# Second 512 rows of x in a gated MLP on one core: eight transposing DMAs, or plain loads turned by TensorE

## The chip, the cores and the metric

The kernel runs on one core of a Trainium2 chip. The metric is the device time of one execution in microseconds (us); of several runs the median counts. All times of instructions come from one profiled execution of the kernel before.

## The reference

```python
B, S, Dm, Df = 1, 2048, 1024, 3584        # all inputs bf16, output bf16
def reference(x, w_gate, w_up, w_down):
    g = jnp.einsum("bsd,df->bsf", x, w_gate)
    u = jnp.einsum("bsd,df->bsf", x, w_up)
    h = jax.nn.gelu(g, approximate=True) * u
    return jnp.einsum("bsf,fd->bsd", h, w_down)
```

## The kernel before, in words

**Passes and units.** The 2048 rows of x are done in two passes of 1024 rows. A pass first makes the hidden layer `hT` for its rows (fourteen units, each with 256 of the 3584 hidden columns) and then multiplies it by `w_down` (`down`). The two 512-row halves of a pass are called c = 0 and c = 1; `xT[0]` and `xT[1]` hold them transposed, the contraction on the partitions.

**Seven products in place of eight.** A unit is a 2x2 block product, for gate and for up, done with seven block products and sums of operands. `sums_t` makes the sums of x: `t1` to `t4`, and `tb`, a cast; they are made once for a pass. `sums_s` makes those of the unit's weights: `s1` to `s4` and `sa`. Sums are kept in fp32r. The block products are the calls of `product` and `first_product` in `unit`; each is four matmuls of 128x512 for gate and four for up, all issued at line 111 in the helper `matmul`.

**The very first unit is plain.** Unit 0 of pass 0 is done without the sums, by `plain`, because the operands are still coming. Five warm-up matmuls (line 484) run first. Then `turn` transposes the four row blocks of the first 512 rows on TensorE (line 434, eight 128x128 transposes for each block, into banks 4 to 7), and VectorE or ScalarE copies each block to `xT[0]` (line 435). `plain(bank[0:4], 0, ...)` follows, then `plain(bank[4:8], 1, ...)`. The second 512 rows arrive already transposed: the helper `transposing` (line 438) issues eight transposing DMAs on SyncE's queue, one for each 128 columns of x, behind the loads of the first rows (`xn`) and of unit 0's weights (`wf`).

**Orders.** TensorE, VectorE, GpSimd and SyncE carry out their instructions in the order of the program; in this opening stretch ScalarE does too. DMAs on SyncE's queue are therefore issued in the order written, and one that waits holds back those behind it. Unit 1's weights (`w = load_w(1, nc.scalar, pinned=True)`) come by ScalarE's queue, issued behind its copy of the second row block. Unit 2's weights also come by ScalarE's queue: `aside(-1)` in unit 1 issues them behind the two snapshots `p1` of `first_product`. Later weights come by SyncE's queue.

**Who makes the sums.** In unit 1 VectorE makes `t` and `s`, ScalarE casts `tb` and `sa`. From unit 2 on GpSimd makes `s1` to `s4` one unit ahead (`make_s(ahead, pool)`). In pass 0 GpSimd also makes the sums of `w_down` in `keep`, tile `m` (one block j of 128 hidden rows of both halves for each unit, the last three at the end, two of them in a weight buffer, where the profile calls the tile `w`); `store_made` writes them to DRAM (`td`) a unit later, and `down` reads them back. The loads of `w_down` that `down` needs (`raw`, line 319) stand on SyncE's queue, some of them behind the last of these stores.

**Pools.** `k` has 52 slots of 2 KB for a partition and holds the row blocks `xn`, the sums, the snapshots and the gelu results; `w` has three weight buffers. A new tile waits until the readers of the slot's last tile are done.

Of the kernel before, what the change touches and what calls it, by code (L numbers as in the profile page):

```python
# [10 lines left out]
def kernel(  # L11
# [23 lines left out]
    nc = tc.nc  # L35
    ENG = mybir.EngineType
    ORDER = {ENG.SP, ENG.DVE, ENG.Pool, ENG.PE}
    P = nc.NUM_PARTITIONS
    bf16 = mybir.dt.bfloat16
# [6 lines left out]
    x2 = x.flatten_outer_dims()  # L46
# [4 lines left out]
    NKB = Dm // P  # L51
# [3 lines left out]
    N = 512  # L55
    NS = N // P
# [19 lines left out]
    def new_x():  # L76
        return [xpool.tile([P, NKB, N], bf16, name=f"xT{c}") for c in range(2)]
# [36 lines left out]

    def load_w(u, queue=nc.sync, pinned=False):
        f0 = u * 2 * P
        w = wpool.tile([P, 2, NKB, 2 * P], bf16, name="w")
        for i, src in enumerate((w_gate, w_up)):  # L120
            got = queue.dma_start(
                out=w[:, i],
                in_=src[:, f0 : f0 + 2 * P].rearrange("(ko ki) f -> ki ko f", ki=P),
            )
            if queue is not nc.sync and not pinned:
                tc.keep_in_program_order(got)
        return w

# [7 lines left out]
    def sums_t(xT):  # L136
        K = range(KH)
        lo, hi = [[xT[c][:, k] for k in K] for c in range(2)], [
            [xT[c][:, KH + k] for k in K] for c in range(2)
        ]  # L140
        return Sums(
            how={
                "t1": lambda q: [new(dve, lo[1][k], lo[0][k], SUB, "t1") for k in K],
                "t2": lambda q: [new(dve, hi[1][k], q["t1"][k], SUB, "t2") for k in K],
                "t3": lambda q: [new(dve, hi[1][k], lo[1][k], SUB, "t3") for k in K],
                "t4": lambda q: [new(dve, hi[0][k], q["t2"][k], SUB, "t4") for k in K],
                "tb": lambda q: [cast(hi[1][k], "tb") for k in K],
            }
        )

    def sums_s(w, eng):
        GU = range(2)
        sh = [P, KH, P]
        a11, a21 = [[w[:, i, :KH, h : h + P] for i in GU] for h in (0, P)]
        a12, a22 = [[w[:, i, KH:, h : h + P] for i in GU] for h in (0, P)]
        return Sums(
            how={
                "s1": lambda q: [new(eng, a21[i], a22[i], ADD, "s1", sh) for i in GU],
                "s2": lambda q: [new(eng, q["s1"][i], a11[i], SUB, "s2", sh) for i in GU],
                "s3": lambda q: [new(eng, a11[i], a21[i], SUB, "s3", sh) for i in GU],  # L160
                "s4": lambda q: [new(eng, a12[i], q["s2"][i], SUB, "s4", sh) for i in GU],
                "sa": lambda q: [cast(a22[i], "sa", sh) for i in GU],
            }
        )
# [257 lines left out]
    def load_x(c):  # L422
        t = []
        for i in range(NS):
            xn = slot([P, Dm], bf16, "xn")
            r0 = c * N + i * P
            nc.sync.dma_start(out=xn, in_=x2[r0 : r0 + P, :])
            t.append(xn)
        return t

    def turn(xT, xn, c, i, copy):
        tp = bank[4 + i].bitcast(bf16).rearrange("p (k r) -> p k r", k=NKB)
        for ko in range(NKB):
            nc.tensor.transpose(tp[:, ko, :], xn[i][:, ko * P : (ko + 1) * P], ident)
        copy(out=xT[c][:, :, i * P : (i + 1) * P], in_=tp)

    def transposing(xT, c, ko, r0):
        nc.sync.dma_start_transpose(
            out=xT[c][:, ko, :], in_=x2[r0 : r0 + N, ko * P : (ko + 1) * P]
        )  # L440

    def load_wf(queue, k0, k1):
        for i, src in enumerate((w_gate, w_up)):
            got = queue.dma_start(
                out=wf[:, i, k0:k1],
                in_=src[k0 * P : k1 * P, 0 : 2 * P].rearrange(
                    "(ko ki) f -> ki ko f", ki=P
                ),
            )
            if queue is not nc.sync:  # L450
                tc.keep_in_program_order(got)

    xT = new_x()
    xn0 = load_x(0)
    wf = wpool.tile([P, 2, NKB, 2 * P], bf16, name="w")
    for k0, k1 in ((0, 2), (2, 5), (5, NKB)):
        load_wf(nc.sync, k0, k1)
    for ko in range(NKB):
        transposing(xT, 1, ko, N)

    def plain(ps, c, kos, parts=1):
        n = N // parts
        for k in range(kos.start, kos.stop, 2):
            for part in range(parts):
                cols = slice(part * n, (part + 1) * n)
                for p, (j, i) in zip(ps, [(j, i) for j in range(2) for i in range(2)]):
                    for ko in (k, k + 1):
                        matmul(
                            p[:, cols],
                            wf[:, i, ko, j * P : (j + 1) * P],  # L470
                            xT[c][:, ko, cols],
                            ko == 0 and part == 0,
                            ko == NKB - 1,
                        )

    def finish(ps, c):
        for j in range(2):
            times(j, c, gelu(ps[2 * j]), ps[2 * j + 1])

    on_dve, on_act = nc.vector.tensor_copy, nc.scalar.copy  # L480
    t = sums_t(xT)
    with tc.manual_schedule(engines={ENG.Activation}):
        for _ in range(NWARM):
            nc.tensor.matmul(bank[3], lhsT=warm[:, :P], rhs=warm, start=True, stop=True)
        for i in range(NS):
            turn(xT, xn0, 0, i, on_act if i == 1 else on_dve)
        w = load_w(1, nc.scalar, pinned=True)
        s = sums_s(w, dve)
        plain(bank[0:4], 0, range(0, 2), parts=2)
        plain(bank[0:4], 0, range(2, NKB))  # L490
        t.make("t1")
        finish(bank[0:4], 0)
        s.make("s1", "s2")
        t.make("t2", "t3", "tb")
        s.make("s3", "sa")
        plain(bank[4:8], 1, range(NKB))
        finish(bank[4:8], 1)
# [8 lines left out]
    for ip in range(NPASS):  # L506
        for u in range(1 if ip == 0 else 0, NU):
            js = making(u) if ip == 0 else []

            def prepare():  # L510
                nonlocal ahead
                nxt["w"], nxt["s"] = ahead, None
                if u + 1 < NU:
                    nxt["s"] = make_s(ahead, pool)
                if u + 2 < NU:
                    ahead = load_w(u + 2)
                if ip == 0:
                    fetch_wd(making(u + 1))
                    for j in making(u - 1):
                        store_made(j)  # L520
                for j in js:
                    keep(j, j != js[0])

            def aside(part):
                nonlocal ahead
                if ahead is None:
                    ahead = load_w(2, nc.scalar)
                if part == 0 and "s4" not in s:
                    s.make("s4")
                    t.make("t4")  # L530

            def ahead_of_p4():
                if u + 1 < NU:
                    nxt["p1"] = first_product(even if u % 2 else odd, xT, nxt["w"])

            e = odd if u % 2 else even
            p1 = nxt.pop("p1", None) or first_product(e, xT, w)
            unit(u, (e, cc, dd), xT, w, s, t, p1, prepare, aside, ahead_of_p4, ip == 0 and u == 1)
            if u + 1 < NU:
                w, s = nxt["w"], nxt["s"]  # L540

        last = ip == NPASS - 1
        got, nxt = {}, {}

        def more(step):

            nonlocal ahead
            if last:
                return
            if step == 0:  # L550
                xT[:] = new_x()
                for j in making(NU - 1):
                    store_made(j)
            if step >= 16 and step % 2 == 0 and step // 2 - 8 < len(moves):
                c, ko = moves[step // 2 - 8]
                transposing(xT, c, ko, (2 * (ip + 1) + c) * N)
            if step == 50:
                got["w"], ahead = load_w(0), load_w(1)
            if step == 58:
                got["s"] = make_s(got["w"], dve)  # L560
            if step == 62:
                got["t"] = make_t(xT)

        down(ip, even + cc, dd + odd, last, more)
        even, odd, cc, dd = odd, even, dd, cc
        if not last:
            w, t, s = got["w"], got["t"], got["s"]
# [29 lines left out]
```

## Time and profile before

| what | value |
|---|---|
| median of 3 runs | 555.94 us (555.9 to 557.38) |
| profiled execution, its own time | 557.38 us |
| its span, first to last instruction | 555.5 us |
| TensorE busy | 539.2 us, 97% |
| VectorE, ScalarE, GpSimd busy | 325.1, 243.5, 279.4 us |
| TensorE's waits for DMAs of `raw` | 10.5 us, 3 times, the longest 9.3 us |
| mean DMA rate | 168 GB/s |

The profiled execution is the longest of the three runs shown; 1.9 us of its time lie outside the span. A busy share is an average: what a change in the opening is worth depends on what the opening hands on, and to which engine.

### The profile page before, as it was taken

The numbers are of one execution on the slowest core, as the hardware profiler recorded it, in microseconds if no ns is written. First come the engines' busy times: TensorE is split into PE (matmuls) and PEld (weight loads), VectorE is DVE, ScalarE is ACT, GpSimd is POOL, SyncE is SP. The second block draws the span as 40 slices with busy tenths as digits, with TensorE's granted clock in tenths as the row PEclk, the third lists the DMA queues.
The fourth block names the chain that finished last, engine by engine and source line by source line (L and its number), as shares of the span: only waits on it lengthen the run. The fifth ranks groups of instructions, "written<-read, shape, count | busy, mean of one in ns | idle before, by whom it ended". The sixth has DMA issues, their size and how long they took to land.

```text
span 555.5 us, 7315 instructions
## 1 busy us (share of the span) xinstructions
PE 539.2 (97%) x2405; PEld 380.1 (68%) x2405; DVE 325.1 (59%) x490; ACT 243.5 (44%) x427; POOL 279.4 (50%) x248
## 2 busy tenths in 40 slices
PE   8999999999999939999999999999999999999997
PEld 5477776676777514788877777766767776478885
DVE  3884555545554892468675445555555548866730
ACT  2555554555555201045435555545555551114541
POOL 0069999999999620000059666777777700000000
PEclk9999999999999969999999999999999999999999
DMA  9884767766634589999925333222222049563751
GB/s 212 164 229 124 201 188 196 201 189 171 170 101 165 203 295 353 265 252 250 327 65 150 100 106 99 77 76 77 76 77 76 0 141 370 190 225 84 223 194 53
DMA packets 108133, 93.28 MB, mean 168 GB/s; under 512 B 17216, under 2 KB 92992, under 8 KB 108096
## 3 DMA queue, kind: packets, MB, share of 16 engines
q1 hardware_dynamic: 103936, 90.72, 56.7%
q10 hardware_dynamic: 4160, 2.10, 1.5%
q8 instruction: 19, 0.31, 0.2%
q14 instruction: 18, 0.15, 0.1%
HBM read 74.45 MB, written 15.20 MB: 161 GB/s over the span
## 4 chain that ended last, share of the span: by engine, by line
PE 61%; DMA 3%; POOL 1%; issue 1%; ACT 0%; SPq 0%; POOLq 0%
PE bank L111 61%; DMA raw<-in_w_down_dram 2%; POOL w L93 1%; DMA td<-w 1%; POOL m L93 1%; DMA td<-m 1%; ACT st L398 0%; SPq L280 0%; POOLq L93 0%
## 5 line engine op out<-in xcount | busy, mean ns | idle before, releaser
L93 POOL TENSOR_TENSOR s<-w 128x512 fp32r<-128x512 bf16 x100 | 116.9, 1189 | 158.0 <-DVE t L90 86.6
L111 PE MATMUL bank<-t,s 128*128 128x512 f32 x648 | 157.0, 398 | 0.0
L111 PEld LDWEIGHTS bank<-t,s 128*128 128x128 f32 x648 | 121.8, 188 | 27.6
L107 ACT COPY p<-bank 128x512 f32<-128x512 f32 x124 | 71.5, 589 | 113.4 <-PE bank L111 113.3
L111 PE MATMUL bank<-xT,w 128*128 128x512 bf16 (+1 forms) x504 | 117.2, 380 | 0.0
L90 DVE TENSOR_TENSOR hT<-g,bank 128x512 bf16<-128x512 f32 x112 | 76.7, 687 | 55.7 <-ACT g L178 48.1
L90 DVE TENSOR_TENSOR sum<-bank,p 128x512 f32<-128x512 f32 x54 | 37.3, 691 | 88.9 <-PE bank L111 87.5
L111 PEld LDWEIGHTS <-w 128*128 128x128 bf16 x504 | 45.8, 99 | 59.4 <-issue 12.9
L178 ACT ACTIVATE g<-sum 128x512 f32<-128x512 f32 x81 | 51.3, 633 | 55.1 <-DVE sum L90 53.5
L111 PE MATMUL bank<-raw,hT 128*128 128x512 bf16 x224 | 51.7, 392 | 10.5 <-DMA raw<-in_w_down_dram 10.5
L111 PE MATMUL bank<-q 128*128 128x512 f32 x240 | 59.0, 389 | 0.0
L111 PE MATMUL bank<-t,sa 128*128 128x512 f32 x216 | 58.7, 413 | 0.0
L93 POOL TENSOR_TENSOR s<-w,s 128x512 fp32r<-128x512 bf16 x50 | 57.5, 1168 | 0.0
L93 POOL TENSOR_TENSOR s<-s,w 128x512 fp32r<-128x512 f32 x50 | 57.2, 1164 | 0.0
L111 PE MATMUL bank<-tb,s 128*128 128x512 f32 x216 | 53.3, 389 | 0.0
L111 PEld LDWEIGHTS bank<-q 128*128 128x128 f32 x240 | 45.1, 188 | 9.3
L111 PEld LDWEIGHTS <-hT 128*128 128x128 bf16 x224 | 22.3, 100 | 39.5 <-issue 15.3
L111 PEld LDWEIGHTS bank<-t,sa 128*128 128x128 f32 x216 | 40.7, 188 | 10.6
L107 ACT COPY u<-bank 128x512 f32<-128x512 f32 x62 | 35.8, 589 | 24.3 <-PE bank L111 24.3
L111 PEld LDWEIGHTS bank<-tb,s 128*128 128x128 f32 x216 | 40.6, 188 | 8.4
L102 ACT CAST tb<-raw 128x512 fp32r<-128x512 bf16 x28 | 17.2, 628 | 63.0 <-DMA raw<-in_w_down_dram 29.7
L90 DVE TENSOR_TENSOR q<-hT 128x512 fp32r<-128x512 bf16 x56 | 42.1, 752 | 3.4 <-PE bank L111 3.4
(43 smaller groups left out, 460.1 us busy)
## 6 DMA issues: line engine op xcount, KB each, us to landing
raw<-in_w_down_dram SPq DMA_DIRECT2D x80, 256.0 KB, 3.6
q<-td SPq DMA_DIRECT2D x60, 256.0 KB, 5.0
w<-in_w_gate_dram SPq DMA_DIRECT2D x25, 512.0 KB, 4.4
w<-in_w_up_dram SPq DMA_DIRECT2D x25, 512.0 KB, 5.9
td<-m SPq DMA_DIRECT2D x12, 768.0 KB, 4.5
w<-td SPq DMA_DIRECT2D x6, 1024.0 KB, 9.0
out_dram<-st SPq DMA_DIRECT2D x32, 128.0 KB, 1.7
td<-w SPq DMA_DIRECT2D x2, 768.0 KB, 3.8
```

The lines of the kernel that those rows point to most:

```text
L90: nc.vector.tensor_tensor(out=out, in0=a, in1=b, op=op)
L93: nc.gpsimd.tensor_tensor(out=out, in0=a, in1=b, op=op)
L102: nc.scalar.copy(out=t, in_=src)
L107: nc.scalar.copy(out=t, in_=ps)
L111: nc.tensor.matmul(ps, lhsT=lhs, rhs=rhs, start=start, stop=stop, skip_group_check=True)
L178: nc.scalar.activation(g, src, ACT.Gelu_apprx_tanh)
```

## The change

The second 512 rows of x come like the first: four plain loads of 128 rows each (`load_x(1)`, tile `xn`), turned by 32 transposes on TensorE and copied to `xT[1]`, two blocks by VectorE and two by ScalarE. The transposes stand inside the plain product of the first rows, two blocks after its first four contraction blocks and two after its sixth. Unit 1's weights move from ScalarE's queue to SyncE's, behind these loads. On VectorE `s1` of unit 1 now stands ahead of unit 0's gated product `hT`, and `s2` behind `t2`. After this opening the instructions of all engines are the same in both kernels, in the same order.

```diff
-    for ko in range(NKB):
-        transposing(xT, 1, ko, N)
+    xn1 = load_x(1)
+    w = load_w(1)
...
-    t = sums_t(xT)
+    s, t = sums_s(w, dve), sums_t(xT)
...
             turn(xT, xn0, 0, i, on_act if i == 1 else on_dve)
-        w = load_w(1, nc.scalar, pinned=True)
-        s = sums_s(w, dve)
         plain(bank[0:4], 0, range(0, 2), parts=2)
-        plain(bank[0:4], 0, range(2, NKB))
+        plain(bank[0:4], 0, range(2, 4))
+        for i in range(2):
+            turn(xT, xn1, 1, i, on_act if i % 2 else on_dve)
+        plain(bank[0:4], 0, range(4, 6))
+        for i in range(2, NS):
+            turn(xT, xn1, 1, i, on_act if i % 2 else on_dve)
+        plain(bank[0:4], 0, range(6, NKB))
         t.make("t1")
+        s.make("s1")
         finish(bank[0:4], 0)
-        s.make("s1", "s2")
-        t.make("t2", "t3", "tb")
+        t.make("t2")
+        s.make("s2")
+        t.make("t3", "tb")
         s.make("s3", "sa")
         plain(bank[4:8], 1, range(NKB))
         finish(bank[4:8], 1)
```

The other lines of the diff write out the helpers `transposing` and `load_wf` where they were called (the transposing DMAs of pass 1's rows stay as they are) and drop the parameter `pinned`.

## The prediction

> **What bounds the kernel now.** I read the page's totals first, then the chain that ended last, then the opening and GpSimd in the timeline.
>
> ```profile
> PE 539.2 (97%) x2405; PEld 380.1 (68%) x2405; DVE 325.1 (59%) x490; ACT 243.5 (44%) x427; POOL 279.4 (50%) x248
> ```
>
> TensorE is busy for 97%, so time added to it anywhere looks like time added to the end. The chain of waits, in order of time, corrects this:
>
> ```profile
> 184.88 1.17 POOL m L93
> ...
> 193.18 1.60 POOL w L93
> ...
> 197.93 4.34 DMA td<-w
> ...
> 202.70 11.26 DMA raw<-in_w_down_dram
> 213.96 0.04 issue
> 214.00 338.08 PE bank L111 x1504
> ```
>
> Columns are start, length, what. From 214 us to the end TensorE never waits. Before that the chain is not TensorE's: GpSimd's sums of `w_down`, their stores, and the loads of `raw` behind those stores. TensorE sits idle there for 10.5 us (9.35 in one piece). So a delay of TensorE in the opening reaches the end only if GpSimd's chain is delayed too. Where does that chain begin?
>
> ```profile
> 24.84 0.37 ACTq L121 DMA_DIRECT2D w<-in_w_gate_dram  x1
> 25.24 0.61 ACTq L121 DMA_DIRECT2D w<-in_w_up_dram  x1
> 32.09 1.16 POOL L93 TENSOR_TENSOR s<-w 128x512 fp32r<-128x512 bf16 x1 [30.79 <-DMA w<-in_w_gate_dram]
> 33.91 1.15 POOL L93 TENSOR_TENSOR s<-w 128x512 fp32r<-128x512 bf16 x1 [0.66 <-DMA w<-in_w_up_dram]
> ```
>
> GpSimd starts on unit 2's weights when they land. The timeline of GpSimd shows no idle time from 33.91 until 180.41: eight sums of `s` and three of `m` fill 12.60 us, exactly TensorE's time for a unit (its sets of `bank<-t,s` start at 38.77, 51.37, 63.97). Whatever delays the landing of unit 2's up weights passes through to 214 us. These two DMAs are issued at 24.84 because they stand on ScalarE's queue behind the `p1` snapshots (the second starts at 24.83), which wait for TensorE's first product of unit 1. TensorE in the opening:
>
> ```profile
> 1.19 2.32 PE L484 MATMUL bank<-warm 128*128 128x512 bf16 x5 [1.19 <-DVE warm L418]
> 3.30 1.91 PE L434 MATMUL bank<-ident,xn 128*128 128x128 bf16 x16
> 6.35 1.89 PE L434 MATMUL bank<-ident,xn 128*128 128x128 bf16 x16 [1.14 <-DMA xn<-in_x_dram]
> 8.03 18.49 PE L111 MATMUL bank<-xT,w 128*128 128x256 bf16 x88
> 33.64 1.90 PE L111 MATMUL bank<-xT,w 128*128 128x512 bf16 x8
> ```
>
> After 8.03 there is no gap. The eight transposing DMAs held nobody up on TensorE, so their removal gives it nothing back.
>
> **The transposes.** 32 are added in that dense stretch, all ahead of the `p1` snapshots. The only row for such a matmul is that of the first rows: 16 in 1.91 us, each 0.31 long, so (1.91 - 0.31) / 15 = 0.107 us apart. That is a slow stretch: the warm-up matmuls of 512 columns are (2.32 - 0.63) / 4 = 0.42 us apart, against (1.90 - 0.38) / 7 = 0.217 at 33.64. (The granted clock reads 1.00 in both, so the pace is read from the spacing.) In the trace the pace doubles at 10.1 us, inside the first `plain` matmuls; the new transposes start at about 12.5. In the slow stretch a transpose takes a quarter of a 512-column matmul, which its 128 columns explain; weight loads hide. At the fast pace a quarter is 0.054. So the bounds are 32 x 0.054 = 1.7 us and 32 x 0.107 = 3.4 us. A gain is excluded: nothing leaves TensorE, and no gap is left to fill. I take 0.055, nearest to the row of the same stretch: **+1.8 us**.
>
> Here the Trainium skill speaks against this change. The page "TensorE: Matmul & The Clock Gate", section "Part 4: PE-mode transpose", says that transposes take about 275 ns in a kernel and that the full clock does not engage for them. The row has 314 ns for the length of one, but neighbours overlap. If the slow spacing held for them at any clock, the sum would be the 3.4 us of the upper bound; the 16 here that stood inside the busy time just before the pace doubled speak against it.
>
> **Do the rows arrive in time?** The loads take the places of the transposing DMAs, whose first is issued at 6.32. The DMA windows show 324 to 330 GB/s from 5 to 8 us, and the first 2 MB (x and `wf`) land by about 10.2. At 0.8 us for each 256 KB the four blocks land near 11.0, 11.8, 12.6 and 13.4. TensorE asks for the first at 10.82 + 8 x 0.216 = 12.54 and for the third at 12.54 + 0.9 + 1.7 = 15.2. Cover: 1.5 and 2.6 us; without it, TensorE waits by the difference. `w` follows by 16.7; `s1` wants it near 20. No cost.
>
> **The copies.** ScalarE's copy of a block took 1.01 us, VectorE's 0.69. Behind the last transposes TensorE has eight matmuls (1.73 us), while the last copy needs about 0.2 to drain and 1.01 on ScalarE. Cover 0.4 us, cost nothing. ScalarE loads its gelu table behind the copies (1.28 us), so unit 0's gelu is about 1 us later relative to TensorE; its banks are asked for 5 us later.
>
> **VectorE.** Before, `t1` is done at 16.3, having waited 4.5 us for the transposing DMAs. Now it starts when the last copy ends, near 17.4. From there 21 operations, 0.61 us apart (18 took 10.95 from 16.25), stand before unit 0's last-but-one `hT` is written: 30.3. That `hT` frees bank 5, which TensorE wants for the second half of `s1` x `t1` at 26.17 + 1.8 + 1.85 + 0.93 = 30.7. Cover 0.4 us; if an operation were 0.03 us slower, it would be gone. Further on, `s4` is ready at 33.4 against 33.6 + 0.9 for its second half, `t4` begins at 34.0 against 37.0. Cost nothing, with 0 to 1 us of stall in the range. VectorE is about 2.5 us later in unit 1, and gives it back in unit 2, where it has no sums to make.
>
> **Queues.** ScalarE loses two DMA issues (0.85 us), which held nobody. On SyncE's queue the loads of unit 3 wait for TensorE's release of `wf`, so they move with TensorE; the 9 us for which the transposing DMAs kept that queue are over by 17 in both. Slots of `k` are taken in the same order, four more early and long free: nothing. GpSimd's first sums run beside a busier VectorE; its operations take 1.15 to 1.19 us in the trace, so 8 x 0.015 = 0.1 us, which I add since its chain has no gap.
>
> **Sum.** 1.8 + 0.1 = +1.9 us, on TensorE and, through the `p1` snapshots, on GpSimd's chain alike. The profiled execution had 557.38 us (span 555.5 and 1.9 around it): 559.3 in its terms. It stands 1.4 us above the median, 555.94, and I put the forecast on the median: **557.8 us**.
>
> **Rivals.** (1) The transposes keep the slow spacing, or TensorE waits for a copy or for bank 5: +2.6 to +4.1, about 559.3. For it: the only row of a transpose is the slow one, and two covers are 0.4 us. Against: the pace doubles for 256-column matmuls at once. (2) The delay is swallowed by the 9.35 us hole at the end of pass 0: about 556.4. It needs the landing of unit 2's weights to move by less than TensorE; against it, their issue stands behind snapshots that wait for TensorE. (3) On the other side, not slower: unit 2's weights land faster. They took 7.2 and 8.6 us from issue to use, sharing the DMA engines with unit 3's weights and the first `raw`, and unit 4's late on; unit 1's on the same queue landed in 4.5 and 6.3 by the trace. If the others moved away wholly, the chain would start up to 2.5 us sooner after the issue: 1.9 - 2.5 = -0.6, about 555.3. It decides from 1.9 us of lead on. Against: the others move with TensorE too, except unit 4's weights, which wait for `s4`, and those overlap by under 0.5 us.
>
> **How the numbers follow.** Forecast 60 in 100 (own range +1.3 to +2.6), rival 1 24, rival 2 8, rival 3 5, anything else 3. 0.3% is 1.7 us, about what a measurement of this kernel can tell from no change. The forecast lies just above: some 43 of its 60 are slower, 17 the same. With rival 1 nearly all slower and one other, 0.68 slower; 17 + 8 + 3 or so make 0.28 the same; 0.04 faster. The range from +0.8 to +4.0, 556.7 to 559.9, leaves out rivals 2 and 3 and the tails. The three runs spread over 1.5 us, which is in it.
>
> **What would show it.** In the changed profile: no gap on TensorE from 8 us to the end of `w_down`'s first products; the new transposes about 0.055 apart; the `p1` snapshots, unit 2's weights, GpSimd's first sum and the start of the last long piece of the chain all later by the same 1.8 to 2.0 us (214.0 becomes about 215.9). Wrong: spacing over 0.08; a wait for `xn`, for a copy or for VectorE on TensorE; the hole shorter than 9 us, which means that the chain did not move with TensorE; or a shift at 214 that differs from that at 33.9.

## The result and the profile after

The changed kernel takes 558.76 us (median of 4, 558.51 to 560.13), the kernel before 555.98 beside it: 1.0049 times as long, 95% interval 1.0026 to 1.0072. A second measurement on one chip gave 558.71 against 556.46, 1.0043 (1.0029 to 1.0057). So by the medians the change costs 2.2 to 2.8 us. Its profiled execution took 558.77 us, with a span of 557.0.

The page and the chain of the changed kernel (columns of the chain: start, length, what):

```profile
PE 539.8 (97%) x2437; PEld 380.3 (68%) x2437; DVE 326.2 (59%) x492; ACT 245.4 (44%) x429; POOL 281.3 (51%) x248
```

```profile
186.13 1.17 POOL m L93
...
188.60 1.50 POOL m L93
...
194.75 1.60 POOL w L93
...
199.50 4.32 DMA td<-w
...
207.41 9.40 DMA raw<-in_w_down_dram
...
224.37 329.45 PE bank L111 x1464
```

The totals hardly move. The chain is the same one, 1.25 us later at the first `m` (184.88 before) and 1.57 later at the last store (197.93); the third `m` took 1.50 in place of 1.17. The wait that starts its last long piece is now one `raw` later, so that piece is compared by the row that both have: TensorE's third wait for `raw` ends at 215.34 after, 214.00 before:

```profile
204.57 6.01 PE L111 MATMUL bank<-raw,hT 128*128 128x512 bf16 x16 [10.36 <-DMA raw<-in_w_down_dram]
211.28 3.61 PE L111 MATMUL bank<-raw,hT 128*128 128x512 bf16 x16 [0.69 <-DMA raw<-in_w_down_dram]
215.34 8.79 PE L111 MATMUL bank<-raw,hT 128*128 128x512 bf16 x40 [0.45 <-DMA raw<-in_w_down_dram]
```

The long idle piece, the hole, is 10.36 us in place of 9.35. Now the opening, from the timeline of the changed kernel:

```profile
3.40 2.30 PE L434 MATMUL bank<-ident,xn 128*128 128x128 bf16 x24
10.44 0.62 PE L434 MATMUL bank<-ident,xn 128*128 128x128 bf16 x8 [0.17 <-DMA xn<-in_x_dram]
11.67 0.62 PE L434 MATMUL bank<-ident,xn 128*128 128x128 bf16 x8 [0.60 <-DMA xn<-in_x_dram]
13.85 1.06 PE L434 MATMUL bank<-ident,xn 128*128 128x128 bf16 x16
25.31 0.42 ACTq L121 DMA_DIRECT2D w<-in_w_gate_dram  x1
26.64 5.83 PE L111 MATMUL bank<-t,s 128*128 128x512 f32 x24
31.62 2.49 DVE L90 TENSOR_TENSOR t<-xT,t 128x512 fp32r<-128x512 bf16 x4
32.46 3.79 POOL L93 TENSOR_TENSOR s<-w 128x512 fp32r<-128x512 bf16 x2 [31.16 <-DMA w<-in_w_gate_dram]
```

Two things are to be seen. TensorE waits for the new rows at 10.44 and 11.67, and yet it begins unit 1's `t` x `s` at 26.64, only 0.48 later than before. And GpSimd's first two sums, which took 1.16 and 1.15 us before, stand in one row of 3.79: by the trace the first took 2.67 and the second began at 35.09. The up weights had landed at 34.19. While VectorE ran `t4` from 31.62 to 34.11, GpSimd's sum made hardly any headway: it ended 1.0 us after `t4`, and alone takes 1.16. In the kernel before the same `t4` ran ahead of it:

```profile
26.17 5.82 PE L111 MATMUL bank<-t,s 128*128 128x512 f32 x24
29.53 2.49 DVE L90 TENSOR_TENSOR t<-xT,t 128x512 fp32r<-128x512 bf16 x4
31.94 0.68 DVE L90 TENSOR_TENSOR hT<-g,bank 128x512 bf16<-128x512 f32 x1
```

`t4` ended at 32.02, and GpSimd started at 32.09, when the gate weights had landed.

### The profile page after: what moved, and what is told of

Its sections match the earlier page's. It is cut to its first block, busy times and chain, and to the rows that moved or that the text cites. A ratio compares the mean times of both kernels' runs of the same rounds, so it can differ in the third digit from the quotient of the medians.

```text
span 557.0 us, 7388 instructions
## 1 busy us (share of the span) xinstructions
PE 539.8 (97%) x2437; PEld 380.3 (68%) x2437; DVE 326.2 (59%) x492; ACT 245.4 (44%) x429; POOL 281.3 (51%) x248
## 4 chain that ended last, share of the span: by engine, by line
PE 59%; DMA 4%; POOL 2%; issue 1%; SPq 1%; ACT 0%; POOLq 0%
PE bank L111 59%; DMA raw<-in_w_down_dram 3%; POOL w L93 1%; DMA td<-w 1%; POOL m L93 1%; DMA td<-m 1%; SPq L319 1%; SPq L553 0%; ACT st L398 0%; SPq L280 0%; POOLq L93 0%
## 5 line engine op out<-in xcount | busy, mean ns | idle before, releaser
L93 POOL TENSOR_TENSOR s<-w 128x512 fp32r<-128x512 bf16 x100 | 118.5, 1206 | 157.8 <-DVE t L90 86.8
```

What stands on the lines that cost most here:

```text
L93: nc.gpsimd.tensor_tensor(out=out, in0=a, in1=b, op=op)
```

## The experiments

**The kernel before, again** (no edit).

> The kernel before, unchanged, for a second profile. Its first profile is of an execution of 557.38 us, while the other three took 555.9 to 556.0. Theory A (the opening of that profile is not the usual one): TensorE's pace doubles near 4.7 us, as in the changed kernel's profile, not at 10.1, TensorE reaches the first set of s x t of unit 1 before 26.17, GpSimd's first sum of unit 2 starts about 1.4 us before 32.09, and the time is 555.9. Theory B (the opening is the usual one and the 1.4 us arise later): 26.17 and 32.09 again, to 0.1 us.

Measured: 556.59 us (10 runs, 556.02 to 558.04) beside 556.57 (19 runs, 555.5 to 558.63), so one and the same kernel spreads over 3 us. In its profile the pace doubles at 6.6 us, TensorE begins unit 1's `t` x `s` at 25.78, GpSimd starts at 31.62. Theory A holds in kind, with 0.4 to 0.5 us in place of 1.4. What the early pace wins is partly lost again:

```profile
18.30 2.00 PE L111 MATMUL bank<-xT,w 128*128 128x512 bf16 x8 [0.51 <-DMA xT<-in_x_dram]
20.52 5.62 PE L111 MATMUL bank<-xT,w 128*128 128x512 bf16 x24 [0.22 <-DMA xT<-in_x_dram]
```

These are waits for the transposing DMAs, which the first profile, with its late pace, did not have. Over the profiles of all thirteen executions here, the pace first doubled between 4.1 and 10.8 us.

**Transposes alone**, on the kernel before (`idle_turn` is `turn` without the copy):

```diff
-        plain(bank[0:4], 0, range(2, NKB))
+        plain(bank[0:4], 0, range(2, 4))
+        for i in range(2):
+            idle_turn(xn0, i)
+        plain(bank[0:4], 0, range(4, 6))
+        for i in range(2, NS):
+            idle_turn(xn0, i)
+        plain(bank[0:4], 0, range(6, NKB))
```

> The kernel before with 32 transposes more on TensorE, of the first rows into banks 4 to 7 at the places of the changed kernel's; nobody reads them, nothing else moves. Theory (three costs: transposes, waits for the rows, a stretched first sum of GpSimd): only the transposes are paid, 32 x 0.056 = 1.8 us, so about 557.7 us, and GpSimd's first sum takes 1.16 us. Rival (the transposes are the whole cost of the change): about 558.7. Rival (TensorE had slack here, waiting for the transposing DMAs in the usual opening): under 557.

Measured: 557.93 us beside 556.57, 1.0023 (1.0007 to 1.0040): 1.3 us, between 0.4 and 2.2. GpSimd's first sum took 1.17. So by the medians the transposes are about half of the change's cost. The change's own ratios, 1.0043 and 1.0049, lie above this interval, though the intervals overlap.

**Unit 2's weights early**, on the changed kernel: `ahead = load_w(2)` right behind `w = load_w(1)`.

> The changed kernel with unit 2's weights loaded on SyncE's queue right behind unit 1's, into the third buffer, which is free; ScalarE's queue issues no DMA. Theory (the end is handed on by GpSimd's chain, which starts when these weights land): GpSimd's first sum of unit 2 starts 8 to 13 us before 32.5, TensorE's idle piece at the end of pass 0 shrinks from 10.4 us by several us, and the time falls to 550 to 556. Rival (the time that TensorE gets behind in the opening is what counts, GpSimd just follows): 558.7, within 0.5.

Measured: 561.61 us, 1.0093 (1.0070 to 1.0115). GpSimd did start early, at 19.2, and TensorE's long wait for `raw` did shrink, from 10.4 to 6.9 us. But the kernel got slower, which neither theory had:

```profile
20.87 6.25 DVE L90 TENSOR_TENSOR t<-xT,t 128x512 fp32r<-128x512 bf16 x4
21.84 3.17 POOL L93 TENSOR_TENSOR s<-s,w 128x512 fp32r<-128x512 f32 x2
```

```profile
PE bank L111 <- DMA raw<-in_w_down_dram: 8.2, 4, 6.9
PE bank L111 <- DVE hT L90: 3.0, 1, 3.0
PE bank L111 <- DVE s L90: 2.2, 2, 1.8
```

The second view lists TensorE's waits: total, times, longest. VectorE's four `t` took 6.25 us in place of 2.49, GpSimd's sums 1.6 each in place of 1.13, as if the two engines took turns. TensorE then waited 5.2 us for VectorE. So GpSimd's sums, started in the midst of VectorE's, slowed both. And little was left of GpSimd's early start: done with unit 2's sums at 31.3, it stood idle until 42.0, a wait that the profile puts down to TensorE, and began unit 3's sums 1 us sooner than in the changed kernel (42.96).

**`t3` by GpSimd**, on the changed kernel: `sums_t(xT, pool)`, with the argument used for `t3` alone.

> The changed kernel with the four sums t3 of pass 0 made by GpSimd, which is idle then, in place of VectorE. VectorE is 2.4 us ahead from there on, so its sums t4 end before GpSimd's first sum of unit 2 starts. Theory (that first sum took 2.67 us in place of 1.16 because it ran beside t4): it takes 1.2 us, GpSimd's chain is 0.85 us earlier, the time 557.4 to 557.9. Rival (it waited for the landing of the weights or for a slot): 2.67 again, 558.7. If GpSimd's t3, run beside VectorE's other sums, takes 3 us each, TensorE waits for it and the time goes above 559.

Measured: 561.33 us, 1.0077 (1.0048 to 1.0106). The theory missed; the time went above 559, though GpSimd's `t3` took 1.6 us each and not 3. VectorE won nothing: its `t1`, run beside GpSimd's `t3`, took 5.37 us in place of 2.50. In this execution TensorE also waited 1.7 us for `xn` and fell back to the slow pace, from 7.4 to 10.9 us, so not all of the loss is the two engines' doing. `t4` ran at 34.76 to 37.25; GpSimd's first sum, begun at 34.19, again fell onto it and took 4.07 us. It ended 1.0 us after `t4`, as in the changed kernel (35.13 against 34.11).

**The changed kernel, again** (no edit).

> The changed kernel again, for its spread beside the kernel before on the same chip and a second profile. Theory (the pace of TensorE doubles at a different moment in each execution, 4.7 to 10.2 us, and GpSimd's first sum is stretched by VectorE's t4): median 2.0 to 2.8 us above the kernel before, single executions of both spread over 2 to 3 us; in the profile GpSimd's first sum takes over 2 us again. Rival (the 1.74 us between the two first profiles is the whole effect, the rest is chance): 1.2 to 1.8 us above.

Measured: the 1.0043 above, 2.25 us; five runs from 558.55 to 559.84. In the profile, with the pace doubling late, at 9.7, nothing waits for the new rows, and GpSimd's first sum takes 2.52. The median lies outside the rival's 1.2 to 1.8 us; the interval, 1.6 to 3.2, still touches it.

**No `t4`**, on the changed kernel:

```diff
             s.make("s4")
-            t.make("t4")
+            t["t4"] = t["t2"]
```

> The changed kernel with the four sums t4 of pass 0 left out; the product that reads them reads t2. VectorE then has no long run of sums from SBUF at 31.6 to 34.1 us, and all else stays. Theory (GpSimd's first sum of unit 2 is held up until t4 is through): it takes 1.16 us, the second starts within 0.1 us of the landing of the up weights, both 0.8 to 0.9 us earlier than in the changed kernel, and so are the last sums m near 186 and the end: 557.4 to 558.0. Rival (it is the weights' landing, or the stretch is caught up before the end of pass 0): the end stays at 558.4 to 558.8.

Measured: 557.95 us (7 runs) against 558.71, ratios to the kernel before 1.0034 (1.0023 to 1.0046) and 1.0043. The intervals overlap, so the time alone does not settle it. The profile does, in GpSimd's timeline:

```profile
32.25 1.17 POOL L93 TENSOR_TENSOR s<-w 128x512 fp32r<-128x512 bf16 x1 [30.94 <-DMA w<-in_w_gate_dram]
33.99 1.16 POOL L93 TENSOR_TENSOR s<-w 128x512 fp32r<-128x512 bf16 x1 [0.57 <-DMA w<-in_w_up_dram]
```

The first sum takes 1.17 and the second waits for its weights alone. Counted from TensorE's first `t` x `s`, the chain's first late `m` starts after 158.6 us, against 159.5 and 159.7 in the two profiles of the changed kernel. So VectorE's `t4` made the stretch, and it was not caught up in 150 us. (GpSimd is idle for 4.5 us ahead of that late `m`, for a reason that the profile does not show; that time is 4.45 to 4.50 in every kernel of this table, so it swallows nothing.) Put side by side (all in us, from the traces):

| kernel | `t` x `s` of unit 1 | first sum took | second sum starts | last matmul starts | between the last two |
|---|---|---|---|---|---|
| before | 26.17 | 1.16 | 33.91 | 551.68 | 517.8 |
| before, again | 25.78 | 1.41 | 33.40 | 551.27 | 517.9 |
| transposes alone | 26.11 | 1.17 | 33.69 | 551.80 | 518.1 |
| no `t4` | 26.48 | 1.17 | 33.99 | 551.99 | 518.0 |
| changed | 26.64 | 2.67 | 35.09 | 553.42 | 518.3 |
| changed, again | 27.58 | 2.52 | 36.03 | 554.50 | 518.5 |
| `t3` by GpSimd | 29.59 | 4.07 | 38.22 | 556.63 | 518.4 |

In these kernels the last matmul starts 517.8 to 518.5 us behind GpSimd's second sum, wherever TensorE stood. Behind TensorE's own `t` x `s` it starts after 525.5 to 525.7 where the first sum was not stretched beyond 1.41, and after 526.8 to 527.0 where it was. By these profiles the stretch costs 1.1 to 1.5 us, 1.3 between the changed kernel and the one without `t4`; by the medians of those two it costs 0.8. Of the 1.3, 0.9 stand at the second sum and 0.3 come at the third late `m`, which took 1.50 us beside VectorE's sums `q` in place of 1.17. (Unit 2's weights early is not in the table: its GpSimd had idle time.) One step of the table stays unexplained: from the end of TensorE's third wait for `raw` to the last matmul it is 337.7 us in both profiles of the kernel before, and 338.0 to 338.1 in all that have the 32 transposes.

**GpSimd relieved**, the same edit on both kernels:

```diff
+        eng = pool if spare else dve
-        pool(m[:, 0], ra[:, N:], ra[:, :N], SUB)
-        pool(m[:, 1], rb[:, N:], m[:, 0], SUB)
-        pool(m[:, 2], rb[:, :N], m[:, 1], SUB)
+        eng(m[:, 0], ra[:, N:], ra[:, :N], SUB)
+        eng(m[:, 1], rb[:, N:], m[:, 0], SUB)
+        eng(m[:, 2], rb[:, :N], m[:, 1], SUB)
...
-                    for j in making(u - 1):
-                        store_made(j)
                 for j in js:
                     keep(j, j != js[0])
+                if len(js) == 1:
+                    store_made(js[0])
```

> The kernel before with the sums m of the blocks j = 0 to 11 made by VectorE, right behind its first hT of the unit, where it idles for 3.1 us of each unit; their store follows in the same unit; j = 12 and 13 stay with GpSimd. GpSimd has 9 us of work for a unit in place of 12.6 and can get ahead. Theory (its saturated chain sets the end of pass 0): its last sums of s are done several us earlier, the last stores too, TensorE's 10.5 us of waiting shrink by 5 us or more, the time is 545 to 551. Rival (TensorE's order sets the end, the hole is that of raw loads alone): 555.5 to 557.

> The same edit on the changed kernel. Theory (with GpSimd no longer saturated only TensorE's own delay is handed on: 1.8 us of transposes and up to 1.1 of waiting for the rows, less up to 1.3 that the kernel before waits for its transposing DMAs): 0.5 to 2.5 us above the same edit of the kernel before, under 554. Rival (the stretched sum costs its 0.9 us here too, on top): 2.5 to 3.5 above it.

Measured: 547.1 and 547.75 us, 0.9830 (0.9815 to 0.9844) and 0.9843 (0.9830 to 0.9857) of the kernel before. TensorE's waits on the kernel before with this edit:

```profile
PE bank L111 <- DMA raw<-in_w_down_dram: 2.7, 3, 1.5
```

They were 10.5 us. GpSimd has idle time again, and its last sums end near 180 us in place of 198. This settles that GpSimd's saturated chain, the sums and the stores behind them, set the end of pass 0; the edit also moves each store a unit earlier, so the two are not told apart. The edit, put on the kernel before, also beats both kernels. In the changed kernel the first sum is still stretched (2.31 us), and with slack on GpSimd the two kernels differ by 0.65 us: the rival's 2.5 to 3.5 is out.

**An interval for that, and the rows sooner.** The last kernel is the changed one with the edit above and:

```diff
     for k0, k1 in ((0, 2), (2, 5), (5, NKB)):
+        if k0 == 5:
+            xn1 += load_x(1, range(2))
...
-    xn1 = load_x(1)
+    xn1 += load_x(1, range(2, NS))
```

> The kernel before with VectorE's m once more, for an interval. Theory: 546.5 to 547.5, the largest spread of the three kernels of this call, because what TensorE waits for the transposing DMAs depends on the moment at which its pace doubles.

> The changed kernel with VectorE's m once more. Theory (what is left of the change once GpSimd has slack is TensorE's own delay): 0.5 to 1.5 us above the other. Rival (TensorE's delay is swallowed here too, by what is left of the hole, 2.7 us): within 0.3 us of it.

> The same, and the loads of the first two row blocks of the second 512 rows stand on SyncE's queue ahead of the last two pieces of unit 0's weights. Theory (where the pace doubles early, TensorE waits 0.2 to 1.1 us for these rows): no wait for them in the profile, the median 0.2 to 0.8 us below after_m_dve_2, and no wait for the weights, which land 1.5 us later but are read 1.7 us after the turned blocks. Rival (the rows never set anything, since TensorE would then wait for the weights or a copy): the same time or 0.3 us more.

Measured: 546.42, 548.43 and 546.83 us; ratios 0.9811 (0.9798 to 0.9825), 0.9843 (0.9828 to 0.9858), 0.9818 (0.9805 to 0.9832). Here the relieved kernels differ by 2.0 us, 0.65 above; over both measurements the medians are 546.85 (9 runs) and 547.79 (8). The first sum is still stretched, to 2.3 to 2.7 us, but now the end follows TensorE: the last matmul starts 515.2 us behind `t` x `s` in both profiles of the kernel before with this edit, and 515.6 in the three of the changed one. So what reaches the end here is TensorE's own delay, by 0.65 to 2.0 us; its size stays open. With the rows loaded sooner 0.4 us are left, within the intervals: in that profile the turned blocks of the second rows wait for nothing, and nothing waits for the weights.

```profile
10.57 1.06 PE L435 MATMUL bank<-ident,xn 128*128 128x128 bf16 x16
11.47 1.89 PE L111 MATMUL bank<-xT,w 128*128 128x512 bf16 x8
13.19 1.06 PE L435 MATMUL bank<-ident,xn 128*128 128x128 bf16 x16
```

The gain of 1.6 us is more than the 0.2 to 0.8 expected. The profile of its partner does not explain it (0.9 us of waits for `xn`, all for the first rows), so how much of it is chance stays open.

## Why the prediction was right, and where it was off

Right: the sign; the chain by which the opening reaches the end (GpSimd's sums, without idle time from unit 2 to 180 us, to the hole at the end of pass 0); the spacing of the new transposes, 0.056 us, in the rows at 13.85; and that no bank or copy makes TensorE wait. The median, 558.76, is 1.0 above the 557.8 forecast. That it came so near is in part luck: one term was mis-sized upwards, another downwards. The prediction wanted the snapshots, GpSimd's first sums and the end of the wait at 214 all later by the same 1.8 to 2.0 us. In the two first profiles the second snapshot moved by 0.47 (24.83 to 25.30), GpSimd's second sum by 1.18 and the end of the wait by 1.34; and one of its signs of being wrong came, a wait of TensorE for `xn`. Four steps were off.

**GpSimd's term, +0.1, was mis-sized: it is about 1, 0.8 by the medians and 1.3 by the profiles.** It was taken from sums that ran beside other work of VectorE. The section on VectorE saw that VectorE would be about 2.5 us later in unit 1 and let that cost nothing, since TensorE had cover. It did not lay this lateness against the engine that bounds, though by its own figures `t4` would begin at 34.0 and GpSimd's first sum at 32.09 + 1.9 = 34.0. In the trace `t4` moved from 29.5-32.0 to 31.6-34.1, onto GpSimd's first sum. The table shows what this costs at the end, the kernel without `t4` shows that it is `t4`, and GpSimd never made it up.

The Trainium skill has the rule for this: the page "Advanced Engine Details and Errata", section "Miscellaneous Facts", says that GpSimd shares a read and a write interface with VectorE and conflicts with VectorE instructions that have two SBUF inputs. The runs agree, with numbers: beside `t` and `s`, whose inputs are both in SBUF, VectorE's 0.62 and GpSimd's 1.13 us for a sum became 1.56 and 1.6, or GpSimd stood still. Beside `hT` and `sum`, which read PSUM, its sums in the units stay at 1.15 to 1.2.

**"The eight transposing DMAs held nobody up"** was true of the profile at hand, not of the kernel. In the second profile TensorE waits 0.7 us for them. **"Do the rows arrive in time?"**, with its cover of 1.5 us, failed for the same reason: the working took the doubling of the pace at 10.1 us as given. In the changed kernel's profile it doubled at 4.7, TensorE reached the rows at 10.3 in place of 12.5, and waited 0.77 us in all for them. The predicted landing times themselves held: 10.4, 11.6, 12.3 and 13.1 against 11.0, 11.8, 12.6 and 13.4.

**The transposes' +1.8** came out as 1.3 (0.4 to 2.2) in the kernel that adds them alone. The interval takes in 1.8. If it is less, part of them may lie in time that TensorE would otherwise wait for the transposing DMAs, as it does in the second profile; no run shows that.

Of the rivals, the first did not come: the transposes were fast, and TensorE waited for no copy and no bank; the wait for the rows is not among its conditions. (Its price, +2.6 to +4.1, takes in the first measurement's 2.8, but for another cause.) The second, a delay swallowed by the hole, did not come either: the hole grew from 9.35 to 10.36 us. The third needed unit 2's weights to land sooner after their issue; they took 7.1 and 8.4 us after, 7.2 and 8.6 before.

The skill's statement that the full clock does not engage for transposes (page "TensorE: Matmul & The Clock Gate", section "Part 4: PE-mode transpose") does not hold here. The first row of the changed kernel's opening above, 24 transposes, has them 0.107 us apart until 4.65 us and, but for one wait for rows, 0.056 from then on. Whether transposes alone would bring the faster pace on, no run shows: the five warm-up matmuls come first in all of them.

## What to carry to other kernels

When an edit makes an engine late, lay its new place in time against the engine that bounds, not only against the one that waits for it: here VectorE had cover towards TensorE, and cost about 1 us through GpSimd. Here an engine without idle time handed its delay on over 150 us, so look for the saturated engine that feeds the last long wait and take work from it; three of its eleven sums for each unit, given to an engine with a gap, were worth 1.7 to 1.9% here. And an opening read from one profile is one draw: ask what it would be at TensorE's other pace.

## What the runs showed of the hardware

The moment at which TensorE's pace doubles varied from 4.1 to 10.8 us between executions with the same first matmuls. The time of one kernel varied over 3 us; how much of that is the pace was not measured.

The hole costs more than its length. In the other kernels the granted clock is halved for some 10 us (6.8 to 13.7) in and behind it: in the rows of the changed kernel above, the first 16 matmuls behind the hole took 6.01 us, the next 16 took 3.61. With the hole gone the granted clock stayed at 1.00 (0.991 before). Counted from `t` x `s`, the kernel before got 10.3 us shorter by relieving GpSimd (525.5 to 515.2). TensorE's waits for `raw` account for 7.8 of it; by an estimate from the 16 matmuls behind the hole, which in the kernel before took 6.15 us against 3.61 for the next, the halved clock accounts for the other 2.5.
